# Holding back the second mask until the first load of w_out has been issued

## The chip, the cores and the metric

The kernel runs on one core of a Trainium2 chip. The metric is the device time of one execution in microseconds (us). Before the change it is 216.28 us, the median of 3 runs (215.97 to 216.39).

A core has a matrix engine (TensorE, called PE in the profile), three engines for elementwise work (VectorE or DVE, ScalarE or ACT, GpSimd or POOL) and a sync engine (SP). Each works through its own instruction list in order; semaphores hold an instruction until what it needs is done. DMA transfers are issued from an engine's list and then run on the core's 16 DMA engines. In this kernel nearly all loads are issued by POOL (the software queue, q0 in the profile), a few at the start by SP and ACT (hardware queues, q1 and q10).

## What is computed

Attention with a sliding window and a few sink positions, followed by a feed-forward block. Cut to what matters:

```python
# q, k, v: 4 batches, 8 heads, 768 positions, 64 per head
scores = q @ k.T / sqrt(64)
keep = (key < 4) | ((0 <= query - key) & (query - key < 128))
a = softmax(where(keep, scores, -1e9))
x = concat_heads(a @ v)                        # 3072 x 512
h = x @ w_in                                   # 512 x 2048
out = (h * sigmoid(1.702 * h)) @ w_out         # 2048 x 512
```

## The kernel before

The 3072 rows are cut into 12 tiles of 256 rows, three for each batch, numbered k = 0 to 11. For each tile the kernel loads q, k and v, casts them to 16 bits where the load has not done so, transposes q and k on PE (L613 and others; later tiles by DMA), copies the transposed blocks out of PSUM, multiplies (L827), takes the exponential on ACT (L865), masks, multiplies with v (L917) and with the sinks' v (L912), normalizes on DVE (L932, L934), transposes the result to xT (L949), and runs the feed-forward block: the products with w_in (mm1, L984), tanh on ACT (L998), the gate on DVE (L1000, into gT) and the products with w_out (mm2, L1163; in the middle tiles L1061, in a scheme of seven products for eight that uses sums wt of blocks of w_out, L1014).

Two masks are built on the chip. The first (`mask`, L342 to L350) is laid out for the tiles whose positions are loaded in pairs, k below 3; `bias` (L354) is made from it. The second (`mask2`) is for tiles k = 3 and on. It takes three operations: a memset to one on DVE (`o_m21`, L365), two selections on POOL that zero what is outside the window (`o_m20`, L361), and a memset on DVE that opens the sink rows (`o_mask2`, L367). In the profile both masks go by the name "mask", since buffer numbers are left out; the lines tell them apart.

Nothing of the order is written out by hand. Every piece of work is an `Op` with the engines that could do it, an estimated duration, dependencies and a priority (a planned due time). `Plan.run` is a greedy planner: it repeatedly takes the operation that can start first by its estimates, on any engine, breaking ties by priority, and so makes a static instruction order for each engine. An operation can have a `behind`: it is not considered until that other operation has been placed. The loads are chained in this way, each behind the one before, in the order of the list `LOADS`:

```python
LOADS = ["a0", "a1", "v0", "b1", "v1", "w0", "w1", "a2", "w2", "w3", "v2", "w4", "w6", "w5", "w7"]
```

Here a0, a1, a2 are q and k of tiles 0 to 2, b1 the second half of tile 1's q and k, v0 to v2 the tiles' v, w0 to w3 four column blocks of w_in (`o_w[0..3]`), and w4 to w7 four row blocks of w_out (`o_w[4..7]`). So `o_w[4]` is the first load of w_out. The loads of tiles 0 and 1's q and k go by SP and ACT without a cast (L555, L567), all others by POOL with the cast (v L500 and L493, w L417, q and k of tile 2 L470, of later tiles L456). The loads b1 (L567, second half) are held by a one-element memset on POOL, `go` (L545), that itself stands behind the loads of v0.

POOL has eight semaphores for the completion of its loads, used in turn: its ninth load waits until its first has landed, and so on. An operation that several engines could do, such as the cast of tile 1's q and k (L312) or the copies of the sinks' keys (`ks`, L312 as well), is given to one by the planner. A line L312 is that of a helper that all copies and casts share; tile names tell them apart.

Because the planner is greedy, an edit to one operation can change the place and the engine of many that follow.

Of the kernel before, what the change touches and what calls it, by code (L numbers as in the profile page):

```python
# [54 lines left out]
class Plan:  # L55
# [4 lines left out]
    def op(self, eng, dur, lat, fn, deps=(), prio=0.0, acq=None, rel=(), kind=""):  # L60
        return self.any({eng: (dur, lat)}, lambda _: fn(), deps, prio, acq, rel, kind)
# [143 lines left out]
def kernel(  # L205
# [159 lines left out]
    o_m21 = op("DVE", 490, 550, lambda: nc.vector.memset(mask2, 1.0), prio=MASK2_AT, kind="const")  # L365
# [33 lines left out]
    o_win, o_wout, o_w = {}, {}, []  # L399
# [822 lines left out]
    loads.sort(key=lambda o: (o.prio, o.seq))  # L1222
    for b_ in range(1, B):
        o_ks0[b_].behind = o_vs0[b_].behind = o_w[5]
    for a_, b_ in zip(loads, loads[1:]):
        b_.behind = a_

# [44 lines left out]
```

## Time and profile before

| | |
|---|---|
| median of 3 runs | 216.28 us (215.97 to 216.39) |
| profiled execution | 216.7 us, span of its instructions 215.0 us |
| PE busy | 207.1 us, 96% |
| DVE busy | 179.2 us, 83% |
| ACT busy | 123.5 us, 57% |
| POOL busy | 72.0 us, 33% |
| granted PE clock | 1.0 throughout |
| data moved by DMA | 25.31 MB in 95100 packets |

The profile is that of one execution. A row of a timeline has the start, the duration, the engine, the line of the kernel (L...), the operation, what it writes and reads, and in brackets the idle time of the engine just before and what ended it. A row of the waits has who waited, for whom, the total in us, how often, and the longest. The chain of work that ended last is followed back from the last instruction through whatever released each step. The rows of DMA queues have packets, MB and the time of the packets as a share of 16 engines over the window asked for; packets overlap, so shares over 100% occur. The busy slices divide the span into 40 parts of 5.4 us, a digit for the tenths.

### The profile page before, as it was taken

What the parts mean: (1) busy time and instruction counts of PE and PEld (TensorE: products, weight loads), DVE (VectorE), ACT (ScalarE), POOL (GpSimd) and SP (SyncE); (2) the same over time, 40 slices, a digit from 0 to 9 for tenths busy, and PEclk for the clock granted to TensorE, in tenths of its full rate; (3) what the DMA queues carried; (4) which work ended last, traced back from release to release, by engine and by line L of the source; (5) the groups of instructions that cost most, each with busy time, mean ns of one, the idle gap of its engine ahead of it and who ended that gap; (6) DMA issues with size and microseconds to landing.
All of it is one profiled execution on the core that took longest, in us unless ns stands there. A gap on an engine that the chain in (4) does not pass through costs nothing.

```text
span 215.0 us, 6078 instructions
## 1 busy us (share of the span) xinstructions
PE 207.1 (96%) x2441; PEld 174.8 (81%) x2441; DVE 179.2 (83%) x416; ACT 123.5 (57%) x255; POOL 72.0 (33%) x101
## 2 busy tenths in 40 slices
PE   7968999999999999999999999999999999999993
PEld 7646888678888888889888987988978988898882
DVE  5668889999889889889869959979959959968684
ACT  4858598247665756646548349347357356545230
POOL 7869738389980080279002190010000000000000
PEclk9999999999999999999999999999999999999999
DMA  6999999999999089699945399991070050020032
GB/s 177 208 167 182 187 190 206 182 153 189 166 162 173 6 76 171 121 98 206 142 135 115 27 84 202 150 183 48 2 119 31 3 146 3 0 96 4 10 112 77
DMA packets 95100, 25.31 MB, mean 118 GB/s; under 512 B 83552, under 2 KB 92256, under 8 KB 95072
## 3 DMA queue, kind: packets, MB, share of 16 engines
q0 software_dynamic: 70912, 12.59, 74.2%
q1 hardware_dynamic: 23072, 11.81, 25.9%
q10 hardware_dynamic: 1088, 0.52, 0.9%
q8 instruction: 19, 0.31, 0.6%
q14 instruction: 9, 0.07, 0.2%
HBM read 27.26 MB, written 6.29 MB: 156 GB/s over the span
## 4 chain that ended last, share of the span: by engine, by line
PE 86%; DMA 7%; POOL 2%; DVE 2%; issue 1%; SPq 0%
PE bank L984 39%; PE bank L1061 30%; PE bank L827 5%; PE bank L917 5%; DMA qk<-in_k_dram 4%; PE bank L1163 3%; DMA xT<-xn 3%; PE bank L912 2%; POOL v L500 1%; DVE osb L1088 1%; PE bank L949 1%; POOL mask L342 1%; PE bank L730 1%; PE bank L672 1%; PE bank L613 0%
## 5 line engine op out<-in xcount | busy, mean ns | idle before, releaser
L984 PE MATMUL bank<-xT,w_in 128*128 128x256 f16 x768 | 101.3, 273 | 0.4 <-DMA xT<-xn 0.4
L998 ACT ACTIVATE th<-bank 128x512 f16<-128x512 f32 x96 | 58.3, 610 | 67.9 <-PE bank L984 65.0
L984 PEld LDWEIGHTS <-w_in 128*128 128x128 f16 x768 | 72.2, 98 | 10.3 <-DMA xT<-xn 0.5
L1000 DVE SCALAR_TENSOR_TENSOR gT<-th,bank 128x512 f16<-128x512 f16 x96 | 64.9, 679 | 5.5 <-ACT th L998 5.2
L865 ACT ACTIVATE at<-bank 128x512 f16<-128x512 f32 (+1 forms) x96 | 49.9, 586 | 2.3 <-PE bank L827 1.8
L1061 PEld LDWEIGHTS <-sm 128*128 128x128 f16 x352 | 33.4, 98 | 4.6 <-issue 0.3
L1061 PE MATMUL bank<-wt,sm 128*128 128x256 f16 x264 | 35.9, 273 | 0.0
L1088 DVE SCALAR_TENSOR_TENSOR osb<-bank,osb 128x256 f32<-128x256 f32 x58 | 23.8, 416 | 12.5 <-PE bank L1061 12.4
L1061 PEld LDWEIGHTS <-gT 128*128 128x128 f16 x264 | 25.0, 98 | 3.4 <-issue 0.2
L493 POOL DMA_DIRECT2D v<-in_v_dram x18 | 15.9, 887 | 31.9 <-PE bank L917 29.7
L1061 PE MATMUL bank<-w_out,gT 128*128 128x256 f16 x176 | 25.3, 273 | 0.0
L879 DVE TENSOR_TENSOR at<-at,mask 128x1024 f16<-128x1024 f16 x30 | 20.4, 680 | 4.7 <-ACT at L865 4.6
L934 DVE TENSOR_TENSOR xn<-bank,rcp 128x256 f16<-128x256 f32 x48 | 20.0, 416 | 0.5
L917 PE MATMUL bank<-v,at 128*128 128x65 f16 x352 | 19.8, 193 | 0.0
L917 PEld LDWEIGHTS <-at 128*128 128x128 f16 x352 | 17.2, 97 | 1.0
L456 POOL DMA_DIRECT2D qk<-in_q_dram x18 | 16.1, 895 | 2.4 <-DVE wt L1014 1.9
L456 POOL DMA_DIRECT2D qk<-in_k_dram x18 | 16.2, 902 | 1.9 <-DMA w_out<-in_moe_w_out_dram 1.6
L1031 DVE TENSOR_TENSOR sm<-gT 128x1024 f16<-128x1024 f16 x22 | 15.1, 687 | 0.3
L827 PE MATMUL bank<-qkT 64*128 64x256 f16 x192 | 13.3, 244 | 0.2 <-DVE qkT L312 0.2
L1061 PE MATMUL bank<-wt,gT 128*128 128x256 f16 x88 | 13.1, 273 | 0.0
L827 PEld LDWEIGHTS <-qkT 64*128 64x128 f16 x256 | 8.1, 94 | 6.1 <-issue 4.6
L1061 PE MATMUL bank<-w_out,sm 128*128 128x256 f16 x88 | 13.0, 273 | 0.0
(70 smaller groups left out, 189.9 us busy)
## 6 DMA issues: line engine op xcount, KB each, us to landing
out_dram<-osb SPq DMA_DIRECT2D x16, 256.0 KB
qk<-in_q_dram POOLq DMA_DIRECT2D x20, 128.0 KB, 6.9
qk<-in_k_dram POOLq DMA_DIRECT2D x20, 128.0 KB, 6.9
v<-in_v_dram POOLq DMA_DIRECT2D x18, 128.0 KB, 6.7
w_out<-in_moe_w_out_dram POOLq DMA_DIRECT2D x4, 512.0 KB, 11.6
out_dram<-osb SPq DMA_DIRECT2D x16, 128.0 KB
w_in<-in_moe_w_in_dram POOLq DMA_DIRECT2D x4, 256.0 KB, 8.3
w_in<-in_moe_w_in_dram POOLq DMA_DIRECT2D x2, 512.0 KB, 9.4
```

The costliest lines, as they stand in the source:

```text
L456: nc.gpsimd.dma_start(cn[:, j, e], src[b, :, t0 + P * j : t0 + P * j + P].rearrange("h p d -> p h d"))
L493: o = op("POOL", ISSUE + 100, (2 * V_NS,), lambda j=j, src=src: nc.gpsimd.dma_start(w16[:, j, :, 0:D], src), war + [o_ones], prio=load_at( ...
L827: nc.tensor.matmul(f32(o_b or o_s, 2 * n + i)[:, c : c + w].rearrange("s (j t) -> s j t", t=P), src[d, j, 1, p], T[d, j0:j1, 0, p], start= ...
L865: nc.scalar.activation(out=A[:, i, 0:W], in_=f32(o_b or o_s, 2 * n + i)[:, 0:W], func=AF.Exp, scale=scale)
L879: nc.vector.tensor_tensor(out=a_, in0=a_, in1=m_[:, 2 * P :].unsqueeze(1).to_broadcast((P, 4, 2 * P)), op=ALU.mult,)
L917: nc.tensor.matmul(avp()[:, j, i], A[:, i, c : c + P], src[:, jj, 2 * p + i, 0:E], start=not r and n == 0, stop=n == len(blocks) - 1, skip ...
L934: o_nn = op("DVE", 333, 425, lambda: nc.vector.tensor_tensor(out=X[:, p].rearrange("s j (h d) -> s j h d", h=2), in0=avp()[:, :, :, 0:D], ...
L984: nc.tensor.matmul(f32(holder[0])[:, bass.ts(e, TB)], w_in16[:, c, bass.ts(Fi, P)], X[:, c], start=(c == 0 and not (halved and e)), stop=( ...
L998: o_t = op("ACT", 477, 600, lambda first=first: nc.scalar.activation(out=th[first.places[0]], in_=f32(first), func=AF.Tanh, scale=0.851), ...
L1000: o_g[k, s] = op("DVE", 595, 690, lambda first=first, s=s: nc.vector.scalar_tensor_tensor(out=g[:, 2 * s : 2 * s + 2].rearrange("p a t -> ...
L1061: nc.tensor.matmul(f32(holder[bank_of])[:, 0:HM], x[:, Fi], w[:, Fi], start=first and Fi == 0, stop=Fi == NH - 1, skip_group_check=True)
L1088: f, ns = (lambda: nc.vector.scalar_tensor_tensor(out=out, in0=src(), scalar=0.5, in1=add, op0=ALU.mult, op1=ALU.add)), (333, 425)
```

## The change

The first of the three operations that build the second mask, the memset `o_m21`, is put behind `o_w[4]`. It is not considered by the planner until the first load of w_out has been placed; the two operations that depend on it follow it.

```diff
     loads.sort(key=lambda o: (o.prio, o.seq))
     for b_ in range(1, B):
         o_ks0[b_].behind = o_vs0[b_].behind = o_w[5]
+    o_m21.behind = o_w[4]
     for a_, b_ in zip(loads, loads[1:]):
         b_.behind = a_
```

The operations concerned, unchanged:

```python
o_m21 = op("DVE", 490, 550, lambda: nc.vector.memset(mask2, 1.0), prio=MASK2_AT, kind="const")
o_m20 = op("POOL", 900, 950, make_mask2, [o_m21], prio=MASK2_AT, kind="const")
o_mask2 = op("DVE", 300, 400, lambda: nc.vector.memset(mask2[0:n_sink, 0 : 2 * P], 1.0), [o_m20], prio=MASK2_AT,
             kind="const")
```

## The prediction, made before the changed kernel ran

> **What bounds the kernel now.** I read the page first (busy shares, slices), then the chain in order of time, then POOL's timeline, since the change moves POOL work, then PE's and DVE's timelines over the first 40 us and the DMA queues microsecond by microsecond.
>
> ```profile
> span 215.0 us, 6078 instructions
> PE 207.1 (96%) x2441; PEld 174.8 (81%) x2441; DVE 179.2 (83%) x416; ACT 123.5 (57%) x255; POOL 72.0 (33%) x101
> PE   7968999999999999999999999999999999999993
> ...
> 3.80 0.82 POOL mask L361 x2
> ...
> 8.03 8.06 DMA qk<-in_k_dram
> ```
>
> PE is full from the fourth slice on: what it has to do after some 17 us is fixed, and the end comes earlier or later by as much as PE's steady stage starts earlier or later. Ahead of that the chain names POOL building the second mask (L361) and one load of k that takes 8.06 us. Where PE stood still:
>
> ```profile
> PE bank L613 <- DVE qk L312: 2.2, 2, 1.1
> SPq L567 <- POOL qk L545: 2.6, 1, 2.6
> ...
> 16.60 0.57 PE L613 MATMUL bank<-ident,qk 128*128 128x128 f16 x7 [1.03 <-DVE qk L312]
> 17.53 0.27 PE L655 MATMUL bank<-qkT,ks 128*128 128x256 f16 x1
> 20.96 1.04 PE L984 MATMUL bank<-xT,w_in 128*128 128x256 f16 x8
> 22.19 1.18 PE L984 MATMUL bank<-xT,w_in 128*128 128x256 f16 x8
> 23.43 3.66 PE L984 MATMUL bank<-xT,w_in 128*128 128x256 f16 x32
> ...
> 16.12 0.43 DVE L312 CAST qk<-qk 128x512 f16<-128x512 f32 x1 [0.84 <-DMA qk<-in_k_dram]
> 17.08 0.39 DVE L312 COPY qkT<-bank 128x512 f16<-128x512 f16 x1
> ```
>
> PE's last stall ends at 16.60: the second half of tile 1's k lands (8.03 + 8.06 = 16.09), DVE casts it in 0.43, PE transposes it. The price of the change is the shift of this point, as far as later gates let it through.
>
> **The change, part by part.** The planner is greedy and replans all that follows, so the instruction order of both kernels is compared. SP's order is the same. PE's is the same from the first product of w_out on; before that a pair of matmuls or transposes changes places here and there. What moves stands in POOL's queue:
>
> ```profile
> 3.80 0.82 POOL L361 TENSOR_SCALAR_AFFINE_SELECT mask<-mask 128x256 f16<-128x256 f16 x2
> 4.57 2.87 POOL L500 DMA_DIRECT2D v<-in_v_dram  x4
> 7.39 0.20 POOL L545 MEMSET qk<- 1x1 f32 x1
> 8.45 0.42 POOL L312 COPY ks<-qkT 64x4 f16<-64x4 f16 x2 [0.85 <-ACT qkT L312]
> 8.81 2.72 POOL L500 DMA_DIRECT2D v<-in_v_dram  x4
> 11.48 2.87 POOL L417 DMA_DIRECT2D w_in<-in_moe_w_in_dram  x4
> 16.64 1.76 POOL L470 DMA_DIRECT2D qk<-in_q_dram  x2 [2.29 <-DMA v<-in_v_dram]
> 25.51 1.64 POOL L417 DMA_DIRECT2D w_out<-in_moe_w_out_dram  x2 [0.16 <-issue]
> 28.90 0.74 POOL L417 DMA_DIRECT2D w_out<-in_moe_w_out_dram  x1 [1.75 <-DMA w_in<-in_moe_w_in_dram]
> ```
>
> 1. *L361 leaves the start.* The first v loads are issued 0.82 us earlier, and so are the one-element memset L545 and the two loads of tile 1's second half, which SP holds for it (2.6 us of SP's waiting above).
>
> 2. *The sink copies go behind the second four v loads.* Those loads no longer wait 0.85 for ACT's copy nor stand behind 0.42 of copies: with item 1 they start near 8.81 - 0.82 - 0.85 - 0.42 = 6.7, some 2.1 us earlier. The w_in loads behind them wait for the first v loads to land, so they gain 0.8 at most.
>
> 3. *When does tile 1's last k land?* These are the software queue (q0, POOL's loads) and SP's queue (q1, tile 1's loads) in the microseconds 6, 8, 10, 12 and 14 of the span, one or two lines each:
>
> ```profile
> q1 hardware_dynamic: 482, 0.24, 91.3%
> ...
> q0 software_dynamic: 996, 0.12, 195.5%
> q1 hardware_dynamic: 81, 0.04, 18.3%
> ...
> q1 hardware_dynamic: 380, 0.19, 108.4%
> ...
> q0 software_dynamic: 988, 0.12, 195.0%
> q1 hardware_dynamic: 82, 0.04, 24.2%
> ...
> q1 hardware_dynamic: 4, 0.00, 1.9%
> ```
>
> SP's queue moves 482 packets a us alone, 380 in the gap between the two bursts of v, and 81 inside a burst. Now the first burst comes 0.82 earlier, into the time in which tile 1 had the engines to itself, and the second follows at once: the gap is gone. Lower bound: the load keeps its 8.06 us and lands 0.82 earlier. Upper bound: its earlier issue gives nothing because packets of the same queue stand before it, and the 0.82 x 482 = 395 packets that passed alone now pass at the mean of the four q1 rates from 6 to 12 shown, (482 + 81 + 380 + 82) / 4 = 256 a us, in 1.54 us: 0.72 later. I take 0.35 later, nearer the upper end: the row of microsecond 14 shows that the load ends in a thin tail of 4 packets a us beside w_in, which the time of its issue does not set.
>
> The Trainium skill's page "DMA: Bandwidth & Descriptors", section "Queues, rings and completion order", says that each DMA engine takes turns between the queues it has work for, packet by packet. By that rule an earlier burst takes turns from SP's queue and the upper end is the right one; the rows of microseconds 8 and 12 agree with it.
>
> 4. *The cast of that k goes from DVE to POOL.* The new order has it there, ahead of the loads of tile 2. No row has a cast of 512 elements on POOL. From below: DVE's 0.43. From above: the two 256-element passes of L361, 0.82. I take 0.75, nearer the POOL row: 0.32 later. The Trainium skill's "GPSIMD Engine Reference", section "Elementwise — side-by-side cycle accounting", has 769 ns for 512 elements; by it the term would be 0.34.
>
> 5. *DVE is free when PE has transposed.* Before, a copy, a normalization and a reciprocal stood between the cast's end at 16.55 and the copy at 17.08, while four transposes take about 0.3 from 16.60. In the new order they run during the wait: 0.1 to 0.18 back, I take 0.1.
>
> 6. *w_in is less late.* The eight products at 22.19 took 1.18, those at 20.96 took 1.04 for the same work: 0.14 of waiting for a half of w_in. A later PE finds it landed: 0.1 back.
>
> 7. *Tile 2's loads wait behind the cast.* They started at 16.64 when v landed; now at the cast's end, 16.09 + 0.35 + 0.75 = 17.2, 0.55 later. Hidden: the queue is full of w_in then, and PE's transposes of tile 2 come at 26.93 (below) against four issues of 0.88, a landing 6.9 after the last (the page's median): 17.2 + 3 x 0.88 + 6.9 = 26.7. The cover is 0.2; what exceeds it stalls PE.
>
> ```profile
> qk<-in_q_dram POOLq DMA_DIRECT2D x20, 128.0 KB, 6.9
> 26.93 0.61 PE L613 MATMUL bank<-ident,qk 128*128 128x128 f16 x8
> ```
>
> 8. *The mask now stands between the first and second load of w_out.* DVE's memset and its last memset, and the gaps in DVE's new place for them:
>
> ```profile
> 2.46 0.48 DVE L365 MEMSET mask<- 128x512 f16 x1
> 5.48 0.27 DVE L367 MEMSET mask<- 4x256 f16 x1
> 26.01 0.69 DVE L1000 SCALAR_TENSOR_TENSOR gT<-th,bank 128x512 f16<-128x512 f16 x1 [0.18 <-ACT th L998]
> 26.88 0.69 DVE L1000 SCALAR_TENSOR_TENSOR gT<-th,bank 128x512 f16<-128x512 f16 x1 [0.19 <-ACT th L998]
> 29.08 0.69 DVE L1000 SCALAR_TENSOR_TENSOR gT<-th,bank 128x512 f16<-128x512 f16 x1 [0.58 <-ACT th L998]
> ...
> DMA to landing us min/median/max: 10.1/11.6/11.6
> 38.30 1.03 PE L1163 MATMUL bank<-w_out,gT 128*128 128x512 f16 x4
> 51.30 0.56 DVE L883 TENSOR_TENSOR at<-at,mask 128x768 f16<-128x768 f16 x1
> ```
>
> The 0.75 of memsets fits into the 0.95 of gaps: nothing. POOL issues the second w_out load about 0.9 later (0.82 and a wait for DVE); the third was held until 28.90 by a landing anyway. The second landed near 26.33 + 11.6 = 37.9, its products stand at 38.30: a cover of 0.4. But over 10 us from issue to landing says that it queues behind other loads, so I cost the delay at nothing; without that cover it is 0.9 - 0.4 = 0.5. The mask's first reader stands at 51.30, over 20 us later: no cost.
>
> Sum: 0.35 + 0.32 - 0.1 - 0.1 = 0.47 us later. The profiled execution took 216.7 (span 215.0 and 1.7 around it), 0.42 above the median of 216.28; its own sum is 217.17, and from the median it is 216.75, 0.22% slower.
>
> **Rivals.** *The chain shortens (faster).* The load keeps its 8.06 us and lands 0.82 earlier, as the chain says. Then -0.82 + 0.32 - 0.1 = -0.6. PE cannot use all of it unless w_in and w_out come earlier too (0.4 of cover at 38.30), so 0.4 to 0.6: 215.8. For it: L361 stands in the chain. Against it: microseconds 8 and 12. It decides if the k load lands before about 15.8.
>
> *It cancels.* The load lands where it did, 16.1: 0.32 - 0.2, so 0.1 later: 216.4. For it: item 3's bounds lie about evenly around zero.
>
> *POOL's queue becomes the bound (much slower).* The cast is held up, by DVE or otherwise, so that tile 2's loads come more than 0.2 beyond the cover of item 7, and w_out's second load misses its 0.4: 0.47 + 0.3 + 0.5 = 1.27 more at the worst, 1.0 as the middle: 217.3. Against it: both are covered by queues that are full. Beside this, the skill's "SBUF — State Buffer", section "Who interferes with whom", has POOL and DVE lock each other out in some modes; no run here shows it.
>
> That the hold does nothing is excluded: the orders differ.
>
> **How the numbers follow.** Forecast 0.40, faster rival 0.25, cancelling 0.18, much slower 0.17. A measurement of this kernel tells about 0.2%, 0.43 us, from no change. The forecast's own range is 216.4 to 217.1; of its 0.40 some 0.12 lie within 0.2%. Faster 0.23 (0.02 of that rival stays inside), within 0.12 + 0.18 + 0.02 = 0.32, slower 0.28 + 0.17 = 0.45. The range runs from the faster rival with a little of the bound of item 3 (215.7) to just above the much slower one (217.5).
>
> **What would show it.** v's first loads at 3.7 to 3.8 on POOL, the second four at 6.7; the k load landing at 16.2 to 16.8; a POOL cast of 0.6 to 0.85; PE's L613 ending its wait near 17.3, and 23.43 turning into about 23.9, with the same distance kept to the end. A k landing near 15.3 or a PE wait at tile 2's transposes or at the second slab of w_out would make it wrong.

## The result and the profile after

The changed kernel took 214.99 us (median; 214.07 to 218.12), the kernel before, measured beside it, 216.26 (215.81 to 217.0). The ratio is 0.9942 with a 95% interval of 0.9924 to 0.9959: 0.58% or 1.27 us faster. It leaves out the execution of 218.12, in which the granted clock was lower (0.992). The forecast was 216.75 with a range of 215.7 to 217.5, so both its sign and its range were wrong.

The profiled execution of the changed kernel took 214.22 us, 0.8 below its median, that of before 216.7, 0.4 above. The 2.5 us between the two spans is therefore twice what the medians say; a second trace of before stands below. The page of the changed kernel, the same rows as shown of before:

```profile
span 212.5 us, 6074 instructions
...
PE 207.0 (97%) x2440; PEld 175.5 (83%) x2440; DVE 179.3 (84%) x416; ACT 122.8 (58%) x254; POOL 72.7 (34%) x102
...
PE   7999999999999999999999999999999999999993
```

PE's work is the same (207.0 against 207.1 us). What went is idle time in the third and fourth slices, 10.8 to 21.5 us, where the digits rise from 6 and 8 to 9. POOL's timeline of the changed kernel:

```profile
3.69 2.91 POOL L500 DMA_DIRECT2D v<-in_v_dram  x4
6.63 0.09 POOL L545 MEMSET qk<- 1x1 f32 x1
6.67 2.71 POOL L500 DMA_DIRECT2D v<-in_v_dram  x4
9.43 0.82 POOL L312 COPY ks<-qkT 64x4 f16<-64x4 f16 x2
10.19 2.83 POOL L417 DMA_DIRECT2D w_in<-in_moe_w_in_dram  x4
13.87 0.60 POOL L312 CAST qk<-qk 128x512 f16<-128x512 f32 x1 [0.84 <-DMA qk<-in_k_dram]
14.42 1.77 POOL L470 DMA_DIRECT2D qk<-in_q_dram  x2
...
21.80 0.68 POOL L500 DMA_DIRECT2D v<-in_v_dram  x1 [0.28 <-DMA qk<-in_q_dram]
22.57 0.76 POOL L417 DMA_DIRECT2D w_out<-in_moe_w_out_dram  x1
23.93 0.77 POOL L361 TENSOR_SCALAR_AFFINE_SELECT mask<-mask 128x256 f16<-128x256 f16 x2 [0.59 <-DVE mask L365]
24.65 0.76 POOL L417 DMA_DIRECT2D w_out<-in_moe_w_out_dram  x1
```

Every issue is earlier than before: the second four v loads 8.81 to 6.67, w_in 11.48 to 10.19, q of tile 2 16.64 to 14.42, the first w_out 25.51 to 22.57. The sink copies wait for nobody any more, since ACT has long made what they copy. The chain of the changed kernel has the last k of tile 1 at 7.16 + 6.56 = 13.72, against 16.09:

```profile
3.73 2.86 POOL v L500 x4
...
7.16 6.56 DMA qk<-in_k_dram
```

PE's timeline of the changed kernel, and one row further on that serves as a mark in all the runs below, the first group of eight products with w_out:

```profile
14.52 0.34 PE L613 MATMUL bank<-ident,qk 128*128 128x128 f16 x3 [0.19 <-POOL qk L312]
...
21.90 2.78 PE L984 MATMUL bank<-xT,w_in 128*128 128x256 f16 x24
...
24.52 0.61 PE L613 MATMUL bank<-ident,qk 128*128 128x128 f16 x8
...
31.37 1.47 PE L984 MATMUL bank<-xT,w_in 128*128 128x256 f16 x12
...
39.05 1.89 PE L1163 MATMUL bank<-w_out,gT 128*128 128x512 f16 x8
```

The same in the profile of before, where the prediction does not show it:

```profile
33.77 1.47 PE L984 MATMUL bank<-xT,w_in 128*128 128x256 f16 x12
...
41.45 1.89 PE L1163 MATMUL bank<-w_out,gT 128*128 128x512 f16 x8
```

The gap is 16.60 - 14.52 = 2.1 us at the transposes and 41.45 - 39.05 = 2.4 at the mark; behind the mark both need the same (173.6 and 173.5 us to the end of the span). So in this pair of traces the whole effect arises in the first 40 us.

### The profile page after: what moved, and what is told of

Read it like the earlier page. It is cut to its first block, busy times and chain, and to the rows that moved or that the text cites. A ratio compares the mean times of both kernels' runs of the same rounds, so it can differ in the third digit from the quotient of the medians.

```text
span 212.5 us, 6074 instructions
## 1 busy us (share of the span) xinstructions
PE 207.0 (97%) x2440; PEld 175.5 (83%) x2440; DVE 179.3 (84%) x416; ACT 122.8 (58%) x254; POOL 72.7 (34%) x102
## 3 DMA queue, kind: packets, MB, share of 16 engines
q0 software_dynamic: 70912, 12.59, 75.1%
## 4 chain that ended last, share of the span: by engine, by line
PE 85%; DMA 6%; POOL 2%; DVE 2%; ACT 2%; issue 1%; SPq 0%; POOLq 0%
PE bank L984 38%; PE bank L1061 29%; PE bank L917 5%; PE bank L827 4%; PE bank L1163 3%; DMA qk<-in_k_dram 3%; DMA xT<-xn 3%; PE bank L912 2%; POOL v L500 1%; DVE osb L1088 1%; ACT at L865 1%; PE bank L949 1%; POOL mask L342 1%; PE bank L613 1%; PE bank L730 1%
## 5 line engine op out<-in xcount | busy, mean ns | idle before, releaser
L1088 DVE SCALAR_TENSOR_TENSOR osb<-bank,osb 128x256 f32<-128x256 f32 x58 | 23.9, 418 | 12.7 <-PE bank L1061 12.5
L912 PE MATMUL bank<-vs,ats 128*128 128x130 f16 x64 | 12.7, 220 | 0.1
```

Source lines behind the costliest of these rows:

```text
L912: nc.tensor.matmul(avp()[:, j].rearrange("s h e -> s (h e)"), As[:, bass.ts(j, P)], vs16[:, b, p].rearrange("s i e -> s (i e)"), start=Tru ...
L1088: f, ns = (lambda: nc.vector.scalar_tensor_tensor(out=out, in0=src(), scalar=0.5, in1=add, op0=ALU.mult, op1=ALU.add)), (333, 425)
```

## The experiments

Three readings of the gain were possible. *A*: the second four v loads, no longer behind the sink copies, bring w_in and the rest of POOL's loads forward. *B*: it is the 0.82 us of L361 at the start of POOL's queue. *C*: it is the new order further on (the cast of k on POOL, the mask beside w_out). A fourth, *D*, is that the profile of before was not typical.

### One part of the change alone

a1: before in its own order, without the two selections.

```diff
-    o_m20 = op("POOL", 900, 950, make_mask2, [o_m21], prio=MASK2_AT, kind="const")
+    o_m20 = op("POOL", 900, 950, lambda: None, [o_m21], prio=MASK2_AT, kind="const")
```

> The kernel before in its own order, with the two selections L361 of the second mask left out and put nowhere else (so the mask of tiles 3 on is not selected; time is read, not the output). The first v loads are issued 0.82 us earlier, the second four still wait for ACT's copy until 8.45. If POOL's start is the chain (theory 1): k of tile 1 lands 0.8 earlier, 15.3, and the end comes 0.6 to 0.8 earlier, ratio 0.9965. If the earlier burst only takes turns from SP's queue (the theory of the prediction): k lands within 0.3 of 16.1 or later, ratio 1.000. If the gain of the change came from the second four v loads (theory 2): ratio above 0.998.

a2: before with L361 in place, the second four v loads put ahead of the sink copies. a3: both edits. a4: the changed kernel again.

```diff
+    ks = next(i for i, (fn, e) in enumerate(order) if fn is o_ks[0, 2].fn)
+    v1 = [o.fn for o in o_cv[1]]
+    order = ([x for x in order[:ks] if x[0] not in v1] + [(f, "POOL") for f in v1]
+             + [x for x in order[ks:] if x[0] not in v1])
```

> The kernel before with all three mask operations where they were, but the second four v loads ahead of the sink copies in POOL's queue (they start at 7.5 in place of 8.81, the copies follow at 10.2). All other orders as before. Theory 2 (the gain comes from the second v loads and with them w_in coming earlier): ratio 0.996. Theory 1: w_in issues can come earlier by no more than the first v landings allow, ratio 0.998 to 1.000. Theory of the prediction: the gap between the bursts goes, k lands later, ratio 1.001 to 1.003.

> Both edits at once: no selections at POOL's start, and the second v loads ahead of the sink copies, in the order of the kernel before, with the cast on DVE. If POOL's queue is all there is to it: the ratio of the changed kernel, 0.994, or 0.001 below since the cast is DVE's. If what the planner changed on PE, DVE and ACT matters: above 0.996.

> The changed kernel again on this chip, for comparison with the three others and for a second profile of it: ratio 0.994; k of tile 1 lands near 13.7 if its 2.4 us of gain belong to the change, up to 1 us later if half of them were that one execution.

| run | median us | ratio to before (95%) |
|---|---|---|
| a1_no_sel | 216.08 | 0.9982 (0.9957 to 1.0006) |
| a2_v1_first | 215.08 | 0.9938 (0.9914 to 0.9961) |
| a3_no_sel_v1_first | 215.01 | 0.9938 (0.9913 to 0.9964) |
| a4_changed_again | 214.78 | 0.9920 (0.9891 to 0.9950) |

The place of the second v loads alone gives the whole gain; removing L361 alone cannot be told from no change. Why not, stands in the trace of a1. POOL's timeline, then PE's:

```profile
9.11 0.41 POOL L312 COPY ks<-qkT 64x4 f16<-64x4 f16 x2 [2.43 <-ACT qkT L312]
...
12.35 2.85 POOL L417 DMA_DIRECT2D w_in<-in_moe_w_in_dram  x4
```

```profile
18.82 0.61 PE L984 MATMUL bank<-xT,w_in 128*128 128x256 f16 x4 [0.68 <-DMA w_in<-in_moe_w_in_dram]
...
20.11 0.61 PE L984 MATMUL bank<-xT,w_in 128*128 128x256 f16 x4 [0.57 <-DMA w_in<-in_moe_w_in_dram]
...
23.25 0.61 PE L984 MATMUL bank<-xT,w_in 128*128 128x256 f16 x4 [0.51 <-DMA w_in<-in_moe_w_in_dram]
```

POOL comes to the sink copies earlier and waits 2.43 for ACT instead of 0.85. The work taken out accounts for about half of the 1.58 us more; the rest is that ACT's copy came later in this execution (the sink copies start at 9.11 in place of 8.45). So the second v loads and w_in are not earlier but later (12.35). The k of tile 1 lands at 12.59, 3.5 us before that of the first profile, and PE's transposes do not wait for it; PE waits 0.68 + 0.57 + 0.51 = 1.76 us for w_in instead.

### Time or order

a5 puts L361's time back into the changed kernel's order, a6 that of the sink copies and their wait, each by memsets of a scratch tile on POOL; a7 takes the cast of k back to DVE; a8 lets the two loads of tile 1's second half go without waiting for POOL.

```diff
# a5: behind the first mask
+        spend(4)
# a6: behind the one-element memset, ahead of the second four v loads
-    lambda h=h: nc.gpsimd.memset(qk32[sl][0:1, h : h + 1], 0.0),
+    lambda h=h: (nc.gpsimd.memset(qk32[sl][0:1, h : h + 1], 0.0), spend(6)),
# both
+    def spend(n):
+        for i in range(n):
+            nc.gpsimd.memset(scratch[:, P * (i % 4) : P * (i % 4) + P], 1.0)
# a7
-    copy(eng, c16[:, :, e, h].rearrange("s i h d -> s h i d"), dst[:, e, h])
+    copy("DVE" if eng == "POOL" else eng, c16[:, :, e, h].rearrange("s i h d -> s h i d"), dst[:, e, h])
# a8
-    GO1 = None, 1
+    GO1 = None, None
```

> The changed kernel with its own order on every engine, and four memsets of a scratch tile (128x128 each, about 0.8 us together) added on POOL after the first mask, where L361 stood: it puts back the 0.82 us of item 1 and nothing else. Theory A (the gain comes from the second four v loads no longer standing behind the sink copies, and with them w_in and all of POOL's later loads): v's first loads start near 4.5, the second four near 7.5, w_in near 10.9, as in the run a2_v1_first, so the ratio to the kernel before stays at 0.993 to 0.995 and the last k of tile 1 lands before 14.8. Theory B (the gain comes from the start of POOL's queue, L361's 0.82 us): all of it is given back, 0.999 to 1.001. Theory C (the gain comes from the order further on: the cast on POOL, the mask beside w_out): 0.992 to 0.994, no difference from the changed kernel.

> The changed kernel with its own order on every engine, and six memsets of a scratch tile (about 1.27 us together) on POOL between the one-element memset L545 and the second four v loads: it puts back the 1.27 us of item 2 (0.85 of waiting and 0.42 of copies) and nothing else; the loads of tile 1's second half are not delayed. Theory A: the second four v loads start near 7.9, w_in near 11.4 as before; the k lands early, as in the run a1_no_sel, but PE then waits for w_in, and most of the gain goes: 0.997 to 1.000. If w_in's place in time is not what counts and an earlier k is enough: 0.992 to 0.995. Theory C: 0.992 to 0.994.

> The changed kernel with the cast of tile 1's last k on DVE in place of POOL (item 4 undone, all else in its place). By its rows the cast on POOL took 0.60 and on DVE 0.43, so 0.17 us or 0.08% less where DVE is free: 0.991 to 0.994. Theory C (the cast on POOL is itself part of the gain, by freeing DVE): 0.995 to 0.998.

> The changed kernel without the one-element memset L545: SP issues the two loads of tile 1's second half without holding them for POOL. Theory A says that the earlier k cannot be used where w_in is next, and that the two loads then share the DMA engines with the first v loads and tile 0's, which come later: the k lands at 12.5 to 13.5 and w_in no earlier than 10.2, 0.992 to 0.998. If the k's landing is the only gate, a landing 1 us earlier brings 1 us: 0.987 to 0.989.

| run | median us | ratio to before (95%) |
|---|---|---|
| a5_pad_start | 214.60 | 0.9929 (0.9903 to 0.9955) |
| a6_pad_v1 | 214.78 | 0.9939 (0.9918 to 0.9959) |
| a7_cast_on_dve | 215.16 | 0.9960 (0.9940 to 0.9980) |
| a8_no_go | 215.68 | 0.9988 (0.9967 to 1.0010) |

a5 speaks against B: with L361's time back, the gain stays. a6 missed what A expected of it: with the second v loads at 7.78 and w_in at 10.97 nothing is lost. Either the start of these loads does not count, or 10.97 is early enough. POOL's timeline of a6, then that of a8 and the row of PE that goes with it:

```profile
7.78 2.73 POOL L505 DMA_DIRECT2D v<-in_v_dram  x4
10.55 0.49 POOL L313 COPY ks<-qkT 64x4 f16<-64x4 f16 x2
10.97 2.91 POOL L422 DMA_DIRECT2D w_in<-in_moe_w_in_dram  x4
```

```profile
9.94 0.71 POOL L417 DMA_DIRECT2D w_in<-in_moe_w_in_dram  x1
12.22 0.70 POOL L417 DMA_DIRECT2D w_in<-in_moe_w_in_dram  x1 [1.57 <-DMA v<-in_v_dram]
13.92 1.50 POOL L417 DMA_DIRECT2D w_in<-in_moe_w_in_dram  x2 [0.99 <-DMA v<-in_v_dram]
```

```profile
14.48 0.45 PE L917 MATMUL bank<-v,at 128*128 128x65 f16 x9 [1.51 <-DMA v<-in_v_dram]
```

In a8 SP issues tile 1's last k at 5.47 in place of 7.16, so that it shares the DMA engines with the first v loads: in microsecond 7 SP's queue moves 333 packets and POOL's 334. The k gains nothing by it (14.15, expected at 12.5 to 13.5; 13.71 in the changed kernel), and v is late. PE then waits 1.51 for v, and since POOL can issue a further load only when one of its last eight has landed, the v that is late holds w_in back by 1.57 + 0.99 as well. Bringing one load forward puts off another. How much of the 1.51 belongs to the edit is open: by the completion records explained below, 15 of the 16 engines had done with that v by 12.90 and the last at 14.44, and this profiled execution (216.71) was the longest of the run's twelve. The run's ratio of 0.9988 lies above the 0.998 that A allowed.

a7 does not come out faster, as the rows of the two casts would have it (0.60 on POOL, 0.43 on DVE), but at 0.996. Its interval overlaps that of a5 and of the changed kernel (0.9942 and 0.9920), and its profiled execution (span 212.5) is as short as the changed kernel's. C had expected 0.995 to 0.998 here; against C stand a2 and a3, which cast on DVE in the old order and have the whole gain (0.9938). Whether the cast on POOL does any good is not settled.

### A second trace of before, and the start of w_in

a9 is the kernel before, unchanged. a10 is before in its own order, with six memsets ahead of the second v loads; a11 is the changed kernel with eleven in place of a6's six; a12 is before with nine between w_in and the loads of tile 2, the place at which the changed kernel has the cast.

```diff
# a10: in the load of tile 1's v, first of four
-    lambda i=i, j=j, src=src: nc.gpsimd.dma_start(
+    lambda i=i, j=j, src=src: (spend(6 * ((k, j, i) == (1, 0, 0))), nc.gpsimd.dma_start(
# a11
-    lambda h=h: nc.gpsimd.memset(qk32[sl][0:1, h : h + 1], 0.0),
+    lambda h=h: (nc.gpsimd.memset(qk32[sl][0:1, h : h + 1], 0.0), spend(11)),
# a12: in the load of tile 2's q and k, ahead of the first
     def f(e=e, i=i, hs=hs, src=src):
+        spend(9 * ((k, c, e, i) == (2, 0, 0, 0)))
```

> The kernel before, unchanged, profiled a second time and timed against itself: 0.998 to 1.002. The question is the landing of tile 1's last k, 16.09 in the first profile of before. If this is what the old order costs (theory A), it lands between 15.5 and 16.7 again and PE's transposes (L613) start near 16.6. If the first profile showed one late DMA engine and not the order (theory D: what counts lies behind, in w_in and the loads after it), it lands at 13.5 to 15 here and PE has another wait in its place.

> The kernel before in its own order, and six memsets of a scratch tile (about 1.2 us) on POOL ahead of the second four v loads: these start near 9.95 in place of 8.81 and w_in near 12.6 in place of 11.48, the loads of k are not touched. If the start of w_in and of the loads behind it sets the end, about 1 us slower: 1.003 to 1.006. If an emptier gap between the two bursts of v lets the k land earlier and that counts, 0.996 to 1.000. If neither counts, but only whether the sink copies stand ahead of the second v loads: 0.999 to 1.001.

> The changed kernel with its own order, and eleven memsets (about 2.2 us) in place of the six of the run a6_pad_v1: the second four v loads start near 8.85, where before had them (8.81), and w_in near 12.0, half a microsecond behind before's 11.48. If the start of w_in sets the end and 10.97 was still early enough: PE waits for w_in as in the run a1_no_sel, 0.998 to 1.002. If it is the order (sink copies behind the second v loads, cast on POOL) and not the time: 0.992 to 0.995.

> The kernel before in its own order, and nine memsets of a scratch tile (about 1.4 us) on POOL between the fourth load of w_in and the first load of tile 2's q: w_in keeps its start near 11.55, and all that POOL issues behind it comes about 1.4 us later. In the changed kernel the cast of k stands at this place and holds the loads of tile 2 back. If the start of w_in is what counts (theory A), nothing is won, 0.999 to 1.002; if w_in also has to be clear of tile 2's loads, which begin to move while it is on the way, PE's waits for w_in shrink and part of the gain appears, 0.995 to 0.998. If the later loads (v, w_out) are what the gain came from, it is slower, 1.002 to 1.006.

| run | median us | ratio to before (95%) |
|---|---|---|
| a9_before_again | 215.93 | 0.9985 (0.9965 to 1.0005) |
| a10_before_pad_v1 | 216.72 | 1.0031 (1.0008 to 1.0054) |
| a11_pad_v1_long | 215.80 | 0.9984 (0.9963 to 1.0005) |
| a12_before_pad_tile2 | 215.88 | 0.9988 (0.9971 to 1.0005) |

a9's trace settles most of it. It is the same program as before, in an execution of 216.09 us, near the median. POOL's timeline and PE's:

```profile
8.53 0.43 POOL L312 COPY ks<-qkT 64x4 f16<-64x4 f16 x2 [1.04 <-ACT qkT L312]
8.90 2.73 POOL L500 DMA_DIRECT2D v<-in_v_dram  x4
11.58 2.87 POOL L417 DMA_DIRECT2D w_in<-in_moe_w_in_dram  x4
...
24.88 0.68 POOL L500 DMA_DIRECT2D v<-in_v_dram  x1 [0.83 <-DMA qk<-in_q_dram]
25.55 1.53 POOL L417 DMA_DIRECT2D w_out<-in_moe_w_out_dram  x2
```

```profile
14.76 0.56 PE L613 MATMUL bank<-ident,qk 128*128 128x128 f16 x7 [0.33 <-DVE qk L312]
...
18.78 0.61 PE L984 MATMUL bank<-xT,w_in 128*128 128x256 f16 x4 [0.38 <-DMA w_in<-in_moe_w_in_dram]
...
22.00 0.61 PE L984 MATMUL bank<-xT,w_in 128*128 128x256 f16 x4 [0.58 <-DMA w_in<-in_moe_w_in_dram]
...
22.67 3.66 PE L984 MATMUL bank<-xT,w_in 128*128 128x256 f16 x32
...
33.17 0.27 PE L917 MATMUL bank<-v,at 128*128 128x65 f16 x3 [0.29 <-DMA v<-in_v_dram]
...
33.63 1.47 PE L984 MATMUL bank<-xT,w_in 128*128 128x256 f16 x12
...
41.31 1.89 PE L1163 MATMUL bank<-w_out,gT 128*128 128x512 f16 x8
```

Here tile 1's transposes come at 14.76, 1.84 us ahead of the first execution (16.60). Follow that lead: after two waits for w_in, 0.38 and 0.58, it is 23.43 - 22.67 = 0.76; after a wait for tile 2's v it is 33.77 - 33.63 = 0.14; and at the mark 41.45 - 41.31 = 0.14. A k that lands 2.5 us earlier brings the old order 0.14 us, because the w_in and v that POOL issues are late by nearly as much. The chain of work of a9 passes through the sink copies and POOL's queue and ends in tile 2's v, not in the k:

```profile
8.53 0.19 POOL ks L312
...
8.96 2.66 POOL v L500 x4
11.62 2.82 POOL w_in L417 x4
14.45 0.81 POOL qk L470
...
24.88 8.25 DMA v<-in_v_dram
```

That v lands at 33.13, and PE's last wait ahead of the mark ends at 33.17. By this chain an earlier w_in alone would have brought nothing in a9: PE would have waited longer for v. Here are the moments at which the 16 DMA engines completed that k, from the completion records in the traces (us of the span; they are single records and stand in no view shown here):

```
run     15 of 16 engines by   last engine
before         13.66             16.09
a9             12.96             13.59
after          12.75             13.71
a4             14.04             14.20
a1             12.37             12.59
a10            12.25             12.58
```

So D is right on the k: 16.09 was one engine of the sixteen, 2.4 us behind the others in one execution. That execution has a late last engine throughout: it is 0.9 to 2.2 us behind the other 15 in each of POOL's first sixteen loads, in a9 0.7 at most. Beside a9 the changed kernel's k (13.71 and 14.20) is 0.1 to 0.6 later, not earlier.

What does follow the change is the start of w_in on POOL and, with it, the landing of the loads from there on. Row by row: the start of the w_in loads on POOL, the landing of the fourth of them and of tile 2's last v (from the completion records), the mark on PE, and the time, in order of the first:

| run | w_in starts, us | fourth w_in lands | last v of tile 2 lands | mark, us | ratio |
|---|---|---|---|---|---|
| a7_cast_on_dve | 9.83 | 19.85 | 30.24 | 39.40 | 0.9960 |
| a3_no_sel_v1_first | 9.84 | 20.00 | 30.21 | 39.89 | 0.9938 |
| a4_changed_again | 9.92 | 20.46 | 30.65 | 39.49 | 0.9920 |
| a8_no_go | 9.94 | 21.19 | 31.39 | 41.52 | 0.9988 |
| after | 10.19 | 19.63 | 30.16 | 39.05 | 0.9942 |
| a2_v1_first | 10.65 | 20.59 | 30.80 | 39.70 | 0.9938 |
| a5_pad_start | 10.66 | 20.20 | 30.61 | 39.64 | 0.9929 |
| a6_pad_v1 | 10.97 | 20.84 | 31.11 | 39.57 | 0.9939 |
| before | 11.48 | 22.71 | 32.92 | 41.45 | 1 |
| a9_before_again | 11.58 | 21.95 | 33.13 | 41.31 | 0.9985 |
| a11_pad_v1_long | 11.60 | 21.38 | 31.78 | 40.11 | 0.9984 |
| a12_before_pad_tile2 | 12.28 | 21.96 | 32.37 | 40.94 | 0.9988 |
| a1_no_sel | 12.35 | 23.21 | 33.40 | 41.94 | 0.9982 |
| a10_before_pad_v1 | 12.61 | 22.15 | 33.34 | 41.66 | 1.0031 |

All that start by 10.97 have the gain, whatever stands ahead of them and whichever engine casts, but for a8: its first w_in load starts at 9.94, the other three only at 12.22 and 13.92, and PE waits for the first v. None that starts at 11.48 or later has it, not even a11 with the changed kernel's own order: 0.9982 to 0.9988 is where the unchanged kernel itself came out (a9, 0.9985). a11 is the only run that separates time from order on this side, and its profiled execution took 214.9 us, the shortest of its twelve: its w_in and v landed ahead of the others of the late group (21.38 and 31.78), hence the mark of 40.11 beside a median of 215.80. No run moves w_in without the loads that POOL issues behind it, so the table does not tell w_in from tile 2's v. Within the first group the start no longer matters. This is how long PE's weight loads waited for w_in in three of the late ones, from the waits of a9, a1 and a10:

```profile
PEld L984 <- DMA w_in<-in_moe_w_in_dram: 1.6, 3, 0.9
```

```profile
PEld L984 <- DMA w_in<-in_moe_w_in_dram: 2.4, 3, 0.9
```

```profile
PEld L989 <- DMA w_in<-in_moe_w_in_dram: 2.1, 4, 0.7
```

The same row has 1.2 in a12, 0.4 in a11 and, behind the late k, 0.2 in before. The waits of the changed kernel have no such row, those of a6, the latest of the first group, one of 0.2. a10, with w_in and tile 2's loads 1.0 us later than in a9 (12.61 and 11.58, 15.41 and 14.38), is the only run that is slower than before: +0.31% or 0.7 us. a12 was meant to keep w_in where it was, but in its profiled execution POOL waited 1.44 for ACT ahead of the sink copies and w_in began at 12.28. It is no slower than a9, though tile 2's loads begin at 16.50 in place of 14.38: these may come 2.1 us later for nothing. Whether w_in gains by their coming later is left open by it, as is what w_in alone is worth.

## Why the prediction was wrong

**What bounds the kernel now.** This is where it failed. "PE's last stall ends at 16.60 ... The price of the change is the shift of this point" took the latest wait of one execution for the gate. That stall was the k's one late DMA engine, and behind it stood two gates of POOL's loads, w_in and tile 2's v, that the late k had covered up: a9 shows them with waits of 0.96 and 0.29 us. So the shift of the stall was not the price of the change; the price lay in the loads behind the sink copies. The row of 1.18 us for eight products at 22.19, read as "0.14 of waiting", was the visible rest of it.

**1, L361 leaves the start.** Right as to the moves: v at 3.69, the memset at 6.63. Worth nothing by itself (a1, 0.9982 with no change inside its interval) and nothing when put back (a5).

**2, the sink copies.** The second four v loads came at 6.67 where 6.7 was forecast. But "w_in ... gain 0.8 at most" was wrong: 11.48 to 10.19 is 1.29, and against a9 it is 11.58 - 9.92 = 1.66 in a4. The landing of the first v, from which the 0.8 was argued, does not hold w_in back in the changed kernel (its row has no wait); POOL simply comes to it earlier. a2 shows that this step alone makes the gain.

**3, tile 1's last k.** Forecast 0.35 later than 16.09; it landed at 13.72. Against the second trace of before (a9, 13.59) it is 0.1 to 0.6 later. The base of 16.09 was wrong; the shift of 0.35 agrees with this but is not shown, since two executions of the old order lie 2.5 apart. SP's queue in the microseconds 8, 10 and 12 of the changed kernel:

```profile
q1 hardware_dynamic: 47, 0.02, 9.6%
...
q1 hardware_dynamic: 317, 0.16, 76.9%
...
q1 hardware_dynamic: 19, 0.01, 4.4%
```

It is starved inside the bursts, 47 and 19 packets, as in before (81 and 82), and has a gap of 317 at microsecond 10. "The gap is gone" was wrong: it now lies between v and w_in, where the sink copies stand. That SP's queue gets less while POOL's has work agrees with the turns between queues of the Trainium skill's "DMA: Bandwidth & Descriptors", section "Queues, rings and completion order". Equal turns, counted in the packets of the profile, they are not: POOL's queue moved 1118 packets beside the 47, while in a8 the two were level (334 and 333). No run here shows what makes the difference, so the working from these rates to a landing is not borne out.

**4 and 5, the cast on POOL.** It took 0.60 against the 0.75 taken, and PE then waited 0.19 for it (0.70 in a4), where it had waited 1.03 for DVE's (0.33 in a9). The 769 ns of the Trainium skill's "GPSIMD Engine Reference", section "Elementwise — side-by-side cycle accounting", are above the 0.60 measured here, and the measurement decides. No run shows that the cast costs anything (a7). Of the 0.1 for a free DVE the rows show next to nothing: from the transposes to the next product L655 it is 17.53 - 16.60 = 0.93 before and 15.43 - 14.52 = 0.91 after.

**6, w_in is less late.** The term that was mis-sized: -0.1 was taken; PE's waits of 0.96 us for w_in in a9 are gone, and a10 shows 0.7 us for 1.0 us of delay of all that POOL issues from the second v on. But by these traces the wait for w_in has no price of its own. In a9 the wait for tile 2's v ends last, and in the other late traces that v landed ahead of its use by less than half a microsecond (an estimate from the landings in the table and the rows of PE: 33.40 and 33.8 in a1, 32.37 and 32.6 in a12, and a wait of 0.2 in a10). So by the traces the gain needs both to come earlier, and both do, since tile 2's last v is issued at 21.80 instead of 24.88 and lands at 30.16 instead of 33.13. The waits of a9 add up to 1.25, close to the 1.27 of the medians, but this is chance: between the traces of a9 and of the changed kernel the mark moves by 41.31 - 39.05 = 2.26 and the time by 216.09 - 214.22 = 1.87. How the gain divides between w_in and v is open.

**7, tile 2's loads.** They were to be 0.55 later and came 2.2 earlier than in the first profile (14.42 against 16.64), level with a9 (14.38). PE's transposes at 24.52 have no wait: covered, as said.

**8, the mask between two loads of w_out.** Right: the second w_out load stands 2.08 behind the first (0.82 before, so 1.26 later where 0.9 was said), and PE has no wait for it up to the mark. PE's order is the same a little less far back than was said: in the changed kernel two of the first products with w_out (L1163, at 33.70) stand ahead of attention products that they follow in before. DVE's two memsets of the changed kernel:

```profile
23.37 0.48 DVE L365 MEMSET mask<- 128x512 f16 x1
...
25.65 0.27 DVE L367 MEMSET mask<- 4x256 f16 x1
```

a3, which has no selection anywhere, is no faster than a4, which has it here (0.9938 and 0.9920).

**The rivals.** "The chain shortens" had the sign and its own condition ("PE cannot use all of it unless w_in and w_out come earlier too"); they did, and this was the point to follow up. It gave 215.8 against 214.99. "POOL's queue becomes the bound" was the wrong way round: in the kernel before, that queue was a bound already, and the change relieves it.

## What to carry to other kernels

A stall that ends last in one execution names a gate, not the only one; where loads are issued by one engine in order, look at what lands next behind it, and take a second trace before a shift is priced by that stall. Waits that stand one behind the other cannot be priced one by one: here, by the traces, w_in and the v behind it had to come earlier together. An instruction that waits, standing in the queue of an engine that issues loads, costs all the loads behind it: here two copies of 0.42 us that waited 0.85 to 1.44 us for ACT were worth more than the 0.82 us of work that was taken out of the same queue. And work removed ahead of such a wait bought nothing that can be told (a1, 0.9982), since the wait takes up what was removed.

## What was not expected of the hardware

One of the 16 DMA engines can finish its share of a load 0.9 to 2.4 us behind the others (before: 13.66 and 16.09 for this k, 17.31 and 18.83 for the first w_in), in one execution and less in the next (a9: 12.96 and 13.59 for the k, 16.76 and 17.41 for the first w_in). The time of a load is that of its last engine, so a single trace can put such a load 2.5 us off the place that the next trace gives it. In a8 the same shows in the first loads of v (12.90 and 14.44 for the fourth). What makes the engine late was not tested.
